# Sketched attention and a multiplicative FFN: the steps behind the sixtieth in another order, with other engines and buffers for some

## The chip, the cores and the metric

One core of a Trainium2 chip runs the whole program. Its engines take instructions in order, each from its own stream: TensorE (PE, and PEld for its weight loads), VectorE (DVE), ScalarE (ACT), GpSimd (POOL) and SyncE (SP), which here issues DMAs. The metric is the device time of one execution in microseconds (us), as the median of the runs shown.

## The reference

```
# attention: q, k, v (4, 4, 1088, 32); S1, S2 (8, 32)
def phi(x):
    a = einsum('rd,bhsd->bhsr', S1, x)
    b = einsum('rd,bhsd->bhsr', S2, x)
    return einsum('bhsi,bhsj->bhsij', a, b).reshape(*x.shape[:-1], 64)
q_p, k_p = phi(q), phi(k)
kv  = einsum('bhsf,bhsd->bhfd', k_p, v)
z   = sum(k_p, axis=2)
num = einsum('bhsf,bhfd->bhsd', q_p, kv)
den = einsum('bhsf,bhf->bhs', q_p, z)[..., None] + 1e-06
x   = (num / den), heads side by side: (4352, 128)
# FFN: w1, w2 (128, 1024), w3 (1024, 1024), w_out (1024, 128)
out = ((x @ w1) * (x @ w2)) @ w3 @ w_out
```

S1, S2 and the weights come as float64 and are read as integer words, from which the program makes float32.

## The kernel before, in words

The work is cut into named steps. A step is a function that issues a few instructions on one engine, and one long string, ORDER, lists all their names. The program calls the steps in that order and then ties each instruction to the one before it on its engine, so that ORDER sets the order on all five engines; an engine waits at an instruction until its data and its buffer are there, and what is behind it waits too. The large loads from SP are tied as well: the fifth is not issued before the first has landed, and so on (UNDER_WAY = 4). A dozen steps named warm are idle matmuls on zeros at the start.

Three more tables go with ORDER. POOL is the set of step names whose elementwise work goes to GpSimd. CPV is the set of copies out of the matmul results that go to VectorE and not to ScalarE. SLOTS says, for each kind of tile, which of its buffers every new tile takes, in the order of the steps; for "x", the three large buffers into which keys (k), values (v) and queries (qh) are loaded, it is one digit for each of these loads.

The names:

- k0 to k3 are the keys of batch 0 to 3. `zero` clears a strip of the key buffer on GpSimd, `load` and `loadr` bring the keys in (lines 560 and 572), `max` is the largest size on ScalarE, `lead` and `rest` (lines 214 and 651) split the keys into two parts, `gram0` to `gram4` are the k Gram products on TensorE (tile ps_g, line 659), followed by small steps on their result (G, T, N, RC), `kp` is the 64-feature product of the keys (line 677), `kv` the product with the values.
- q0 to q3 are 512 queries each, two of them to a batch, q4 and q6 are the 1024 queries of batches 2 and 3, qr the queries left over. `tr` transposes the loaded queries (lines 1000 and 1333), `restT` the left-over ones; then come products (ps_ay, ps_c, ps_cy, ps_a), a split of their results into parts (`sm`, `st`, `sh`, `sl`; s_g, s_t, s_hl), features (ph), and x: ps_xt and ps_xs, copied (`xc`, line 1274) and multiplied into xT (line 1291).
- g0 to g3 are the FFN on 512 tokens of batch 0 and 1 each: `a` is x @ w1 (line 1799), `c` its copy out (line 1804), `b` is x @ w2 (line 1809), `m` the product of both (line 1815), `o` the product with w3o = w3 @ w_out (line 1835; w3o itself is made by f0 to f7, line 534).
- h4 and h6 are the FFN on batches 2 and 3 in a form with seven products for each eight, on 64 x 128 pieces: X, Y, Z (line 1673), elementwise sums (T, m, s, v), P products (128 x 64 pieces, line 1759), and sums of these (k1 to k9, lines 1776 to 1785) with a factor spread by 16 small copies on GpSimd (`ns`, line 1497). gr is the FFN of the tokens left over, 256 columns wide, with its output products at line 1824.
- w1 to w10 are pieces of the weights and of S, loaded (lines 430 to 440) and made float32 in three or four steps each (`c`, `m`, `j`, `a`).

In TensorE's rows a full matmul step is two instructions of 512 columns on the whole 128 x 128 array; X, Y, Z use 64 of its rows, P 64 of its columns, and the k Gram and the query products 32 or 64 rows.

Of the kernel before, what the change touches and what calls it, by code (L numbers as in the profile page):

```python
# [37 lines left out]
        "0123456789aejo96p3ke3rfjo7p5t8g50lfin6q8o4donmgp19fh2og3hi5601au6v4jm8emhubcusv62jgo6olsjs"
        "aolp8s0h8roj26gk1ivl8hb3mcu0a5pn7tfd9qe0umb4p5j1e2tkmgjeno5rcub7tjkume92fka4ud5tkbigpq10lv"
        "e4idunrdbfoedkio782hvo",  # L40
    "q_m": "0110110",
    "raw": "010212120211221",
    "s": "012345671252360063202461521024214",
# [10 lines left out]
    g4.oS g5.oS g6.oS g7.oS h4.0T1 h4.0T2 h4.0T3 h4.0m12 h4.0m22 h4.1T2 h4.1m11 h4.1m12 h4.2m11  # L54
    h4.2m12 h4.2m22 h4.3m11 h4.s2 h4.s4 h6.0T2 h6.0m11 h6.0m12 h6.0m22 h6.1T2 h6.1T3 h6.1m11 h6.1m12
    h6.1m22 h6.2T1 h6.2T4 h6.2m11 h6.3T3 h6.3m11 h6.s1 h6.s2 h6.s4 k0.Nf k0.Nh k0.Nr k0.kp1 k1.Nr
    k1.kp1 k2.kp0 k2.kp1 k2.rest0 k3.kp0 k3.kp1 q0.al q0.p01 q0.phi1 q0.sca q1.al q1.bs q1.p12
    q1.phi q1.sca q2.bs q2.p2 q2.phi0 q2.sc q2.sl q3.al q3.bs q3.p01 q3.p12 q3.p2 q3.phi0 q3.sc
    q4.al q4.bs q4.nn q4.p01 q4.p2 q4.phi0 q4.sl q6.al q6.nn q6.p01 q6.phi1 q6.sc q6.sl qr.al qr.bs
    qr.p12 qr.p2 s.KS s.Pp s.blk s.blkh s.low s.rest  # L60
# [22 lines left out]
q0.al k0.Nf q0.phi0 q0.phi1 q0.A1 q0.smy w1.m1 k1.max q0.sty q0.shy k0.kv3 k0.kv1 k0.kv2 q0.sly s.KS k0.kvr kr1.tr
k0.kvm w1.m0 kr1.kT q0.p01 q1.C0 q1.C1 q0.C1 k0.kzt k2.loadr q0.pt0 q0.C1t q0.scy q0.p2 k0.kz q0.pt1 k0.kvc kr1.ab
k0.kqt q0.p12 q0.dn q0.de q0.rc w1.j0 q0.pc0 q0.pc1 q0.x0 k1.kT0 q0.x1 q0.xs0 q0.xs1 q0.xt0 w1.a0 q1.A0 k2.load
w0.load k1.lead0 q0.xc0 q0.xc1 k0.kq w1.a1 k2.max q0.xt1 k1.ab q0.xT0 q0.xT1 g0.4a q1.load g0.5a q1.sm w0.m1 q1.st
q1.Ct g0.4c g0.4b q1.sh q1.sl k1.rest0 g0.7b w0.c1 g0.7a k1.abt w0.j1 k1.gram0 w0.c0 s.RC q1.scy k1.gram1 kh2.load
q1.sca q2.tr g0.5c q1.al q1.p01 q1.p2 k1.gram2 k1.gram3 kr1.abc k1.gram4 w6.load w0.m0 g0.6b w0.j0 g0.7c g0.7m k1.Gm
q1.p12 k1.Gc g0.0a w2.load w0.a1 q1.dn q1.de q1.rc q1.bs k1.Gt g0.3a k1.Ga k1.T0 k2.kT1 k1.Gb g0.3c q1.restT g0.2a
q1.phi k1.T1 q1.pt0 g0.4m w0.a0 q2.max q2.l2 g0.6a k1.Ta k2.lead0 k2.rest0 g0.1a g0.2c k1.Tc g0.5b q3.tr g0.5m k1.Tb  # L90
q1.pc0 q1.pt1 g0.1b w9.load k1.N0 s.AR q2.l1 q2.rm v3.zero q1.pc1 k1.N1 q1.x g0.6c g0.1c k1.Na k1.Nr k3.zero k2.gram0
g0.1m k2.gram1 k2.gram2 q3.max k2.gram3 g0.0c k2.kT0 k1.Nb q1.xT k2.gram4 q3.l2 k2.ab q2.A0 q2.C0 q2.C1 q3.l1 k1.kp0
v1.zero w9.c k2.abt g1.5a g1.5c g1.1a q2.Ct g1.7a q2.At q3.rm q3.A0 k0.Nr q2.sm q3.C0 q3.C1 k2.Gm v1.loadr q2.st w2.m
q2.sh g1.1c g1.2a k1.kp1 g0.6m q3.Ct g1.0a g1.7b k3.load v1.load g1.5b q3.At k2.Gt k3.loadr w2.c k2.Ga g0.0b w9.j
q2.sl g1.7c w6.c g1.6a k1.kv0 q3.sm k2.Gb w5.load q2.sc q2.al g1.0c k2.Gc g1.7m q2.p01 q3.st k1.kv2 k1.kv3 q3.sh w9.m
k1.kv1 k2.T0 k1.kvr q3.sl q2.p2 k2.T1 q2.p12 q2.dn q2.de g1.4a q2.rc k3.max g0.3b g0.0m g1.1b kh3.load g1.4c k2.Ta
g1.2b q3.sc g1.2c w5.c k2.Tc k1.kvc k1.kqt k1.kq g0.3m q3.p01 g1.6c g1.3a g1.5m g1.3b q2.bs q2.phi0 q2.pT0 g1.2m g1.3c
q2.x q2.load k2.N0 k2.Tb k3.lead0 w9.a1 k2.N1 g1.4b q3.al q3.p2 q3.p12 q2.xT0 g2.5a k3.kT1 g2.5c g2.6a q3.dn q3.de
k2.Na g1.3m g2.4a g2.3a w5.m g2.4b g2.6c k3.rest0 g1.0b k2.Nr q3.rc g1.1m g1.4m g1.6b k2.Nb g0.2b kr1.kp w6.j q4.tr
g2.4c g1.6m w7.load w7.c q3.bs q4.max q2.restT w6.m w5.j w2.j q4.l2 w3.load w9.a0 k3.gram0 k3.gram1 k3.gram2 q3.load  # L100
w7.j q3.phi0 k3.gram3 k3.gram4 g2.2a k3.Gc g2.1a g1.0m w2.a0 g2.6b g2.0a g2.4m g2.1c f6.t w6.a0 w4.load g2.3b w2.a1
g2.2b g2.2c g2.0c w6.a1 g2.1b q3.pT0 k3.Gm g0.2m k3.Gt k3.kT0 v3.load w7.m f6.m w5.a1 w5.a0 g2.3c k3.Ga k3.Gb g2.3m
w7.a0 g2.1m w3.m g2.6m q3.x k3.T0 k3.T1 f2.t w3.c w3.j w8.load g2.0b q3.xT0 g3.1a f6.o k3.Ta g3.0a g3.0b g2.7a g2.7b
q4.l1 w7.a1 q4.rm g3.0c g3.0m g2.5b v3.loadr g3.3a w4.c g2.0m g2.2m g3.1c g2.5m g2.7c g2.7m v2.zero g3.6a k3.Tb
v2.loadr k3.ab f4.t k3.Tc k3.abt w4.j g3.3c w3.a1 q4.A0 q4.C0 q4.C1 q4.At k3.N0 k3.N1 v2.load w3.a0 f0.t k2.kp1 f4.m
w4.m g3.6c q3.restT q6.tr g3.6b g3.6m q4.Ct q4.sm w10.load f0.m k2.kp0 f4.o g3.1b f0.o g3.1m qr.max q6.max k3.kp1
q4.st k2.kv0 w4.a1 k3.kp0 k2.kv3 k2.kv1 k2.kv2 k2.kvr q4.sh qr.l2 k3.kv0 k3.kv1 f3.t k2.kvc k3.kv3 k3.kv2 k3.Na w4.a0
qr.l1 qr.rm q4.sl q4.sc q4.al k3.kvr k3.kvc g3.4a q6.l2 g3.4c g3.4b q4.p01 k3.Nr g3.3b q6.l1 w8.c g3.5a k3.Nb g2.4o
g3.4m f1.t f3.m w10.c k3.kqt g3.5c w8.m g3.3m q4.p2 q6.rm k3.kq f1.m f1.o q6.A0 q6.C0 w10.j q6.C1 g3.1o f3.o w8.j
q4.p12 q6.At g3.2b w10.m q6.Ct q4.dn g3.7a q6.sm q6.st w8.a0 w10.a0 qr.A0 qr.C0 qr.C1 g3.0o g2.1o g3.7c w10.a1 g0.3o  # L110
qr.Ct qr.At q6.sh q4.de g1.4o q4.rc q4.bs g3.5b q4.na w8.a1 f2.m f2.o q6.sl q6.sc g2.3o f7.t qr.sm g3.5m q4.nb q4.nm
g3.2a qr.st g3.2c g1.6o q4.nr q4.ne q4.nn q4.phi0 g0.2o q6.al k2.kqt f5.t g3.2m f5.m f5.o q4.phi1 q4.pT0 g3.7b g3.7m
qr.sh g3.6o f7.m k2.kq g0.4o q4.pT1 f7.o v.s v.t q4.x q4.xT2 q6.p01 g3.4o q6.p2 g2.7o g1.2o q6.p12 qr.sl g0.6o q6.dn
q6.de g1.5o q4.xT0 qr.sc qr.al q6.rc q6.bs q4.xT1 q6.nb q6.na q6.nm q6.nr q6.ne v.1 q6.nn q6.phi0 q4.xT3 q6.phi1 o.S3
q6.pT0 h4.s1 q6.pT1 g0.1o g0.0o g0.5o g0.7o g1.0o h4.s2 g3.5o g0.oT g1.7o q6.x g1.1o g2.5o qr.p01 qr.p2 qr.p12 qr.dn
g3.3o qr.de qr.rc qr.bs qr.phi0 qr.pT0 g3.2o q6.xT0 q6.xT1 q6.xT2 o.S1 g2.2o v.2 g3.7o q6.xT3 qr.x qr.xT0 g1.3o g2.0o
g1.oT g2.6o h4.1a5 g3.oT h4.0b5 h4.0bd h4.0a1 h4.0ac g2.oT h4.s3 h4.0b1 o.S2 h4.0bc h4.1a1 h4.1ac h4.1b1 h4.0b2 h4.0a2
# [1817 lines left out]
```

## Time and profile before

| | us |
|---|---|
| median of 3 runs (lowest, highest) | 245.7 (245.46, 246.02) |
| span of the profiled execution | 244.1 |
| median less that span | 1.6 |
| TensorE busy | 236.2 |
| VectorE busy | 206.7 |
| GpSimd busy | 161.9 |
| ScalarE busy | 123.5 |

The profile is of one execution. It has its span, from the first to the last instruction, and no other time of its own; the times of the runs hold what lies around the span as well. Busy times are sums over the span, so an engine that is busy for 85% can be the one waited for in some stretch. The granted clock was 0.998 of full speed over the span. Rows of the timeline have start, duration, engine, line, operation, output <- input and shapes; in brackets at the end stands the idle time before, and what ended it.

### The profile page before, as it was taken

To read this page: it belongs to the slowest core of one execution; us is meant where nothing else is said; L and a number is where in the kernel's file an instruction comes from. 1 tells how busy PE (TensorE), PEld (TensorE's weight loads), DVE (VectorE), ACT (ScalarE), POOL (GpSimd) and SP (SyncE) were. 2 spreads that over 40 slices of the span, in tenths; PEclk is the share of its full clock that TensorE was granted. 3 is DMA by queue.
4 is the path that set the end of the run, shared out by engine and by line. 5 is a ranking of instruction groups with operands and counts; after the bars stand their busy time and mean duration, and the time that the engine had idled before them with its cause. 6 is when DMAs were issued, how large, how long until landed. Compare 5 with 4: busy or idle time off the path is not lost.

```text
span 244.1 us, 6745 instructions
## 1 busy us (share of the span) xinstructions
PE 236.2 (97%) x2724; PEld 129.8 (53%) x2724; DVE 206.7 (85%) x421; ACT 123.5 (51%) x246; POOL 161.9 (66%) x203
## 2 busy tenths in 40 slices
...
GB/s 201 265 143 325 181 227 190 6 197 224 220 141 251 188 217 190 59 1 3 3 0 0 4 0 3 59 113 3 1 0 0 0 3 0 0 1 3 12 90 93
DMA packets 31935, 22.06 MB, mean 90 GB/s; under 512 B 21280, under 2 KB 26528, under 8 KB 31904
## 3 DMA queue, kind: packets, MB, share of 16 engines
...
q14 instruction: 10, 0.08, 0.1%
...
## 4 chain that ended last, share of the span: by engine, by line
PE 87%; DMA 5%; ACT 2%; POOL 2%; DVE 1%; issue 1%; POOLq 0%; SPq 0%
PE b_ps L1809 12%; PE ps_o L1835 12%; PE ps_X L1673 11%; PE a_ps L1799 11%; PE ps_o L1759 10%; PE ps_w3o L534 6%; PE ps_Y L1673 6%; PE ps_Z L1673 3%; PE ps_g L659 2%; PE ps_x L1527 2%; PE ps_ac L1374 2%; DMA qh<-in_q_dram 2%; DMA k<-in_k_dram 2%; PE ps_or L1824 2%; POOL ph L1208 1%; PE idle_ps L255 1%
## 5 line engine op out<-in xcount | busy, mean ns | idle before, releaser
L1673 PE MATMUL ps_X<-xd,wv 64*128 64x512 f32 x112 | 36.3, 593 | 0.0
L1799 PE MATMUL a_ps<-xT,w 128*128 128x512 f32 (+1 forms) x80 | 36.1, 562 | 0.0
L1809 PE MATMUL b_ps<-xT,w 128*128 128x512 f32 (+1 forms) x80 | 35.6, 555 | 0.0
L1804 ACT COPY ffa<-a_ps 128x512 f32<-128x512 f32 (+1 forms) x38 | 20.1, 540 | 29.2 <-PE a_ps L1799 26.7
L1707 POOL TENSOR_TENSOR hc<-hc 128x512 f32<-128x512 f32 x16 | 20.7, 1304 | 15.7 <-DVE hc L1685 15.5
L1835 PE MATMUL ps_o<-ab,w3o 128*128 128x512 f32 x64 | 29.6, 600 | 0.0
L1680 ACT COPY hc<-ps_X 128x512 f32<-128x512 f32 x38 | 21.3, 590 | 16.1 <-PE ps_X L1673 12.9
L1815 DVE TENSOR_TENSOR ab<-ffa,b_ps 128x512 f32<-128x512 f32 (+1 forms) x40 | 23.9, 623 | 4.9 <-PE b_ps L1809 4.1
L501 POOL TENSOR_TENSOR w3c<-w3c,cv_m 128x512 int32<-128x512 int32 x16 | 21.2, 1344 | 4.2 <-DVE w3c L495 4.1
L1673 PEld LDWEIGHTS ps_X<-xd,wv 64*128 64x128 f32 x112 | 14.9, 186 | 13.1 <-issue 10.9
L1799 PEld LDWEIGHTS a_ps<-xT,w 128*128 128x128 f32 x80 | 14.1, 189 | 13.9 <-issue 8.8
L1809 PEld LDWEIGHTS b_ps<-xT,w 128*128 128x128 f32 x80 | 14.4, 190 | 13.1 <-issue 8.1
L1673 PE MATMUL ps_Y<-xd,wv 64*128 64x512 f32 x48 | 19.7, 594 | 0.0
L1835 PEld LDWEIGHTS ps_o<-ab,w3o 128*128 128x128 f32 x64 | 11.6, 190 | 13.4 <-issue 13.0
L534 PEld LDWEIGHTS ps_w3o<-wo,w3T 128*128 128x128 f32 x128 | 15.3, 192 | 2.4 <-issue 2.4
L534 PE MATMUL ps_w3o<-wo,w3T 128*128 128x128 f32 x128 | 15.7, 276 | 0.0
L1759 PE MATMUL ps_o<-hc,w3o 128*64 128x512 f32 x32 | 15.1, 595 | 0.0
L1759 PE MATMUL ps_o<-tt,ws 128*64 128x512 f32 x32 | 13.7, 594 | 0.0
L1680 ACT COPY hc<-ps_Y 128x512 f32<-128x512 f32 x14 | 8.1, 592 | 9.7 <-PE ps_Y L1673 6.6
L263 ACT ACTIVATE cv_c<-raw 128x1024 f32<-128x1024 f32 (+1 forms) x13 | 13.0, 1014 | 0.0
L1540 ACT COPY xd<-ps_x 64x256 f32<-64x256 f32 x24 | 8.8, 367 | 7.2 <-PE ps_o L1835 6.8
L1497 POOL COPY nz<-nz 32x8 f32<-32x8 f32 x32 | 11.1, 347 | 1.4
...
## 6 DMA issues: line engine op xcount, KB each, us to landing
...
```

Source lines behind the costliest of these rows:

```text
L263: act.activation(dst, hi.bitcast(F32), ACT.Prelu, scale=2.0 ** -112, alpha=-2.0 ** 32)
L501: pool.tensor_tensor(d, d, x["m"][:, i * 512:(i + 1) * 512], ALU.add)
L534: pe.matmul(t["o"], w3T[ko][:, c], wo[:, c], start=c == 0, stop=c == NC - 1)
L1673: pe.matmul(x[bank], stat(j, u)[:, i * 128:(i + 1) * 128], rows(j, u), start=new, stop=True, tile_position=(u * 64, 0), skip_group_check=True)
L1680: cp(n(y))(x[k], x[bank])
L1707: on(f"h{g}.{i}m{k}").tensor_mul(both[0][k], both[0][k], both[1][k])
L1759: pe.matmul(acc_o[bank][half[0]:half[1]], w(i), x(i), start=n == 1, stop=n == (2 if j == 3 else 4), tile_position=(0, half[0]), skip_group ...
L1799: pe.matmul(x["a"][:, :w], w_of(0, c), xT[g][:, c0:c0 + w], start=True, stop=True)
L1804: cp(f"g{g}.{c}{su}c")(x["s"][:, :w], x["a"][:, :w])
L1809: pe.matmul(x["b"][:, :w], w_of(1, c), xT[g][:, c0:c0 + w], start=True, stop=True)
L1815: dve.tensor_mul(ab_sb[g, c][:, c0:c0 + w], x["s"][:, :w], x["b"][:, :w])
L1835: pe.matmul(o_ps[g], w3o[:, c], ab_sb[g, c], start=n == 1, stop=n == NC)
```

## The change

The four tables get new values; no step's code changes, and with one line more in ORDER all line numbers are one higher. The first sixty or so steps stay where they are. Behind them the order is new, made by a search that started from the old order. POOL has 89 names in place of 90: 26 names in, 27 out. CPV has 23 in place of 17. In the diff a row of SLOTS stands for the tables:

```
-    "x": "012012201110",
+    "x": "012012101102",
```

From the fifth tile of this kind on, other loads come to other buffers: the keys of batch 2 took the buffer of the keys of batch 0, and take now the one of the queries of batch 1.

On SP, the first loads behind the keys of batch 1; the rows are loads in the order of issue, k being keys (a whole batch, 128x4x256, and its left-over part, 64x4x32), kh keys with another layout, v values, qh queries, raw weights. Before:

```order
L560 DMA k<-in_k_dram 128x4x256
L572 DMA k<-in_k_dram 64x4x32
L609 DMA kr_436<-in_k_dram 64x4x32 x2
L572 DMA k<-in_k_dram 64x4x32
L560 DMA k<-in_k_dram 128x4x256
L430 DMA raw<-in_moe_w_dram 128x512 x2
L975 DMA qh<-in_q_dram 128x1088
```

And now:

```order
L561 DMA k<-in_k_dram 128x4x256
L573 DMA k<-in_k_dram 64x4x32
L431 DMA raw<-in_moe_w_dram 128x512 x2
L594 DMA v<-in_v_dram 64x4x32
L976 DMA qh<-in_q_dram 128x1088
L602 DMA kh<-in_k_dram 32x1024 x4
L441 DMA raw<-in_moe_w_dram 32x4x256 x4
L573 DMA k<-in_k_dram 64x4x32
L561 DMA k<-in_k_dram 128x4x256
```

The two loads of batch 2's keys stood right behind those of batch 1 and ahead of the queries of batch 1; they stand now behind these queries and two more loads.

On DVE, the rows that end with the first x (xT); ay_C, s_loy, s_pr, s_d, s_rc belong to the first queries, s_g, s_t, s_hl and a second ay_C to the next ones, qT to batch 1's. Before:

```order
L1068 STREAM_TRANSPOSE ay_C_601<-ps_cy 128x128
L1101 TENSOR_TENSOR s_loy<-s_loy,ay_C_601 128x128
L1180 TENSOR_TENSOR s_pr<-s_al,s_loy 128x128
L1184 TENSOR_TENSOR s_pr<-s_pr 128x128
L1189 TENSOR_REDUCE s_d<-s_pr 128x2x16
L1194 SCALAR_TENSOR_TENSOR s_rc<-s_d 128x16
L1198 RECIPROCAL s_rc<-s_rc 128x16
L466 TENSOR_SCALAR w_81<-cv_c 128x2x256
L1274 COPY xc<-ps_xt 128x256 x2
L1291 TENSOR_TENSOR xT<-xc,ps_xs 128x256 x2
```

And now, from the same product on:

```order
L1181 TENSOR_TENSOR s_pr<-s_al,s_loy 128x128
L467 TENSOR_SCALAR w_81<-cv_c 128x2x256
L1185 TENSOR_TENSOR s_pr<-s_pr 128x128
L1334 STREAM_TRANSPOSE qT<-qh 128x512
L1190 TENSOR_REDUCE s_d<-s_pr 128x2x16
L1195 SCALAR_TENSOR_TENSOR s_rc<-s_d 128x16
L467 TENSOR_SCALAR w_81<-cv_c 128x2x256
L1199 RECIPROCAL s_rc<-s_rc 128x16
L980 STREAM_TRANSPOSE qT_rest<-qh 128x64
L1131 STREAM_TRANSPOSE ay_C<-ps_c 128x384
L1158 TENSOR_TENSOR s_hl<-ps_a,s_hl 128x2x128
L1275 COPY xc<-ps_xt 128x256
```

The steps of the next queries (L1131, L1158) and two transposes of batch 1's queries (L1334, L980) have come in ahead of xT; one of the two copies xc has gone to ScalarE. Further up, not shown, the first reductions of the next queries and the second kp of batch 0, from GpSimd, have come in as well.

On PE, the end of the program, where the P products of the last batch (64x512) and the FFN of the tokens left over (128x256 and 128x128) stand. Before:

```order
L1824 MATMUL ps_or<-w3o,ab 128x128 x3
L1759 MATMUL ps_o<-hc,ws 64x512 x2
L1824 MATMUL ps_or<-w3o,ab 128x128
L1799 MATMUL a_ps<-xT,w_81 128x256
L1809 MATMUL b_ps<-xT,w_81 128x256
L1759 MATMUL ps_o<-hc,ws 64x512 x2
L1799 MATMUL a_ps<-xT,w_81 128x256
```

And now:

```order
L1760 MATMUL ps_o<-hc,ws 64x512 x2
L1760 MATMUL ps_o<-tt,w3o 64x512
L1800 MATMUL a_ps<-xT,w_81 128x256
L1825 MATMUL ps_or<-w3o,ab 128x128
L1800 MATMUL a_ps<-xT,w_81 128x256
```

Before, the last P products alternated with work on the whole array; now they stand in one piece, and all of the left-over tokens' work here comes behind them.

More of the change, by code (lines that the diff above doesn't have):

```diff
@@ L29 @@
     "b":
-        "012345670214657210671306537457462512346127340273014526045721472352140327540542370673245716"
-        "210605643174306437107523543106572361507514502371054643535436051532410354273245554744570504"
-        "7734023146507073701426351241254057163771361764573436046273673572571236574127105",
+        "012345670214567201573102637514031624504625406712061547021734756027416053274164053261405360"
+        "512640357104257610727325031425670312567312574160352604127641324763512476324763132713421213"
+        "6472310547236435654263107637360473521232513142172503460504361746713526074153762",
     "k_g": "0101",
     "l":
-        "0123456789a7486797c0864b7705995a34210b38c73b92bc0b4879c146a281ba56271a564b60303643a19ca32c"
-        "c2076b",
-    "m":
[L38 to L43, printed above, removed]
-    "x": "012012201110",
+        "0123456789abc12057483a6c0b9528617a0b417c638c0156b0785c9243864b137894b2630ac78a241965c7a308"
+        "2967ac",
+    "m":
+        "0123456789abcdefghijklmnopqrstuv24013567ca8jblptqio9efgh5cp16s3bua84dmol73sb458a1uf1ns0a1i"
+        "s52ue7bnh4t2p3170vi9eajc5n8sh6gkqlufmordc1hvuk5lmpr3h075tjr2uhvf6pcqd87k03ljmgovfkdhlim51s"
+        "qepu9kdear63tgfmqivj2o",
+    "q_m": "0101010",
+    "raw": "012012021021201",
+    "s": "012345672540137620541730625147637",
+    "x": "012012101102",
 }
@@ L53 @@
 POOL = set("""
[L54 to L60, printed above, removed]
+    g4.oS g5.oS g6.oS g7.oS h4.0T1 h4.0T2 h4.0m11 h4.0m12 h4.0m22 h4.1T2 h4.1T4 h4.1m11 h4.1m12
+    h4.1m22 h4.2T3 h4.2m12 h4.2m22 h4.3T2 h4.3m11 h4.s1 h4.s3 h4.s4 h6.0T1 h6.0T2 h6.0m11 h6.0m12
+    h6.0m22 h6.1T1 h6.1T3 h6.1m11 h6.1m12 h6.1m22 h6.2m11 h6.2m22 h6.3T1 h6.3T4 h6.s1 h6.s2 h6.s3
+    h6.s4 k0.Nf k0.Nh k1.Nr k1.kp0 k2.kp1 k3.kp0 k3.kp1 q0.al q0.p01 q0.phi1 q0.sca q1.al q1.bs
+    q1.p01 q1.phi q1.sca q1.scy q2.al q2.p01 q2.p2 q2.phi0 q2.sc q3.p01 q3.p12 q3.phi0 q4.al q4.nn
+    q4.p01 q4.p12 q4.p2 q4.phi1 q4.sc q6.al q6.nn q6.p12 q6.phi0 q6.sc qr.al qr.bs qr.p01 qr.p12
+    qr.phi0 s.AR s.KS s.Pp s.blk s.blkh s.low s.rest
 """.split())
@@ L83 @@
[L83 to L117, printed above, removed]
@@ new lines @@
+k0.gram1 k0.ab0 k1.load q1.max q0.C0t k1.loadr k0.gram2 k0.gram3 k0.gram4 s.Pp k0.abc1 q0.sha w1.c0 kr0.abc k0.kp1
+q0.sla kr1.tr warm8 kr1.kT k1.tr1 k0.Gm k0.Gt w1.c1 q1.l2 q1.l1 kr0.kp w0.load k0.Gc k0.abc0 k0.Ga k0.T0 q1.rm k1.tr0
+k0.Ta k0.N0 k0.Gb k1.kT1 k0.T1 q0.sca k1.max v0.loadr k0.Tb k0.Tc q1.C0 q1.load q0.al k0.N1 w1.m0 s.KS warm9 warm10
+warm7 k1.kT0 kr1.ab k0.kp0 k0.Na k0.Nh q1.A0 k1.lead0 k0.Nb q0.phi0 k0.Nf q0.A1 w1.m1 k0.kv0 q0.smy kh2.load k0.kv3
+q0.sty q0.C1 k0.kv1 q1.sm k0.kv2 k0.kvr q0.shy q0.phi1 q0.C1t q0.pt0 q1.st k0.kvc q0.p01 q0.sly q0.pt1 s.AR k0.kvm
@@ new lines @@
+k0.kzt q0.pc0 q1.sh q0.scy q0.p2 q1.C1 w1.j1 q0.p12 q2.tr k0.kz q0.dn q0.de q0.pc1 w1.j0 q0.x0 w0.m1 w1.a1 q0.x1 k1.ab
+q0.rc w1.a0 q1.restT q0.xc0 q1.Ct q1.sl q1.sca q0.xs0 q0.xt0 q0.xc1 q0.xs1 q0.xT0 q0.xt1 k0.kqt warm11 q0.xT1 k3.zero
+q2.max q3.tr g0.5b q3.max q1.scy w9.load q1.p01 k1.abt k1.rest0 g0.5a k2.zero g0.7b k0.kq w0.c0 g0.6a k1.gram0
+k2.loadr k2.kT1 k2.load g0.5c w0.m0 w0.c1 w0.j1 k1.gram1 q1.al q1.p2 g0.5m k1.gram2 k1.gram3 s.RC q1.p12 w0.a1 w9.m
+k3.loadr w9.c w0.j0 w7.load k1.gram4 g0.6b k1.Gm g0.2a g0.6c g0.4a k0.Nr k2.max q1.dn k3.load k1.Gc g0.0a q1.de g0.3a
```

88 lines of the change are left out of this document (57 added, 31 removed).

## The prediction

> **What bounds the kernel now.** I read the page's first part, then the busy time by stretch, then the chain of work that ended last, then each engine's rows where TensorE stops. The page's line gives TensorE nearly the whole span, and the stretches (start and end, length, then busy time with instruction counts of PE, PEld, DVE, ACT, POOL, granted clock, DMA share, GB/s) say where it isn't busy:
>
> ```profile
> PE 236.2 (97%) x2724; PEld 129.8 (53%) x2724; DVE 206.7 (85%) x421; ACT 123.5 (51%) x246; POOL 161.9 (66%) x203
> ...
> 10.38:27.27 16.89, 15.24 (x412) 12.53 (x409) 12.85 (x41) 13.29 (x30) 11.06 (x18) 1.00 0.73 224
> 27.42:47.90 20.48, 19.08 (x382) 10.20 (x390) 18.21 (x44) 15.05 (x30) 12.40 (x17) 1.00 0.66 160
> 47.91:240.40 192.49, 192.49 (x1844) 100.03 (x1828) 170.22 (x320) 89.25 (x171) 134.27 (x136) 1.00 0.28 65
> ```
>
> From 47.91 to 240.40 TensorE never stops, at a full clock. There only its own work counts. So the time can move in three places: how early the first FFN product starts (27.42), what TensorE waits for between 27.42 and 47.90 (20.48 − 19.08 = 1.40 us), and what its work behind that costs. The profiled execution's span is 244.1; the median of the runs shown is 245.7, 1.6 above it. I sum against the span and add the 1.6.
>
> The chain (start, duration, work) gives the prices of TensorE's steps:
>
> ```profile
> 44.27 1.56 PE ps_g L659 x75
> 45.83 1.16 issue
> 46.98 0.54 PE ps_g L659 x15
> 49.17 2.77 PE a_ps L1799 x6
> 67.78 3.43 PE a_ps L1799 x8
> 76.47 1.91 PE a_ps L1799 x4
> 159.41 1.72 PE ps_X L1673 x8
> ```
>
> The first three rows are batch 2's k Gram with a stall in it. Of the FFN rows two instructions are one step. A 512-column step on the whole array takes 3.43/4 = 0.86, one on a 64-row half 1.72/4 = 0.43. Where such a row starts behind another tile shape it is longer: 2.77 against 3 × 0.858 = 2.57, and 1.91 against 1.72: 0.2 for leaving and coming back, 0.1 for each switch of shape.
>
> **The change, part by part.** No instruction is added or taken away; 1 step fewer lies on GpSimd and copies change engine. The counts of matmuls of each shape stay, so TensorE's work without switches stays.
>
> *The first FFN product.* It needs the first x, which DVE makes. DVE's rows on the way (idle time before a row, and who ended it, in brackets):
>
> ```profile
> 14.91 0.19 DVE L217 TENSOR_REDUCE G_g<-ps_g 128x1 f32<-128x32 f32 x1 [1.35 <-PE ps_g L659]
> 16.63 1.21 DVE L677 TENSOR_TENSOR kp<-kab 128x1024 f32<-128x1024 f32 x1
> 18.96 0.16 DVE L937 TENSOR_TENSOR RC<-RC,ps_Nr 128x8 f32<-128x8 f32 x1 [0.41 <-PE ps_Nr L912]
> 23.20 0.32 DVE L1068 STREAM_TRANSPOSE ay_C<-ps_cy 128x128 f32<-128x128 f32 x1 [1.38 <-PE ps_cy L1030]
> 25.71 0.74 DVE L1274 COPY xc<-ps_xt 128x256 f32<-128x256 f32 x2
> 26.48 0.79 DVE L1291 TENSOR_TENSOR xT<-xc,ps_xs 128x256 f32<-128x256 f32 x2
> 27.19 0.42 DVE L1137 TENSOR_REDUCE s_g<-ps_a 128x32 f32<-128x256 f32 x1
> 27.64 0.42 DVE L201 SCALAR_TENSOR_TENSOR s_t<-s_g,ps_a 128x256 f32<-128x256 f32 x1
> 27.98 0.57 DVE L1130 STREAM_TRANSPOSE ay_C<-ps_c 128x384 f32<-128x384 f32 x1
> 28.48 0.41 DVE L204 SCALAR_TENSOR_TENSOR s_hl<-s_g,s_t 128x256 f32<-128x256 f32 x1
> 28.92 0.42 DVE L1157 TENSOR_TENSOR s_hl<-ps_a,s_hl 128x256 f32<-128x256 f32 x1
> 32.32 0.70 DVE L1333 STREAM_TRANSPOSE qT<-qh 128x512 f32<-128x512 f32 x1
> 37.03 0.22 DVE L979 STREAM_TRANSPOSE qT_rest<-qh 128x64 f32<-128x64 f32 x1
> ```
>
> From 10.38 to the end of xT at 27.27, DVE works 12.85 and idles 4.04. The change puts ahead of xT what stood behind it or elsewhere: the second kp (1.21 on DVE), the five rows of the next queries (0.42 + 0.42 + 0.57 + 0.41 + 0.42 = 2.24), the transposes of 0.70 and 0.22, and one small copy, taken as the 0.16 of RC's row. One of two xc copies leaves, 0.37. That is 1.21 + 2.24 + 0.92 + 0.16 − 0.37 = 4.16 more. If none of it falls into idle time x is 4.16 later; if all 4.04 are filled, 0.1. I go through the order: kp and the copy now stand ahead of the reduction that waited 1.35, and fill that; rows of the next queries stand ahead of the transpose that waited 1.38, and fill about 1.1; the 0.41 is behind the second kp and goes. So 2.86 are filled, and the first FFN product comes at 27.42 + 1.3 = 28.7: **+1.3**. The kp that DVE takes was 1.94 on GpSimd:
>
> ```profile
> L677 POOL TENSOR_TENSOR kp<-kab 128x1024 f32<-128x1024 f32 x1 | 1.9, 1943 | 0.0
> ```
>
> GpSimd isn't late for xT in either order, so its relief earns nothing there.
>
> *TensorE's own stall.* The 1.16 in the chain is idle time in which TensorE waited for nothing the profile shows, in the middle of batch 2's k Gram. Its like stands at 14.27 (0.41) and 20.35 (0.91). Between the first two lie 124 + 125 instructions, between the second and this one 505 + 505, some records being lost. I take it for a refill of TensorE's instructions every 256:
>
> ```profile
> 14.26:20.34 6.08, 5.17 (x124) 4.26 (x125) 4.78 (x17) 4.49 (x11) 4.12 (x8) 1.00 0.58 186
> 20.35:46.97 26.62, 24.90 (x505) 14.51 (x505) 22.57 (x61) 19.86 (x41) 15.59 (x19) 1.00 0.70 183
> 43.08:46.97 3.89, 2.75 (x149) 1.80 (x139) 3.79 (x12) 3.31 (x7) 0.49 (x3) 1.00 0.02 4
> ```
>
> The last of these stretches is my count of 256 back from the stall (it also counts those still running at its start). A refill thus took 3.9 us with idle DMA (0.02) and 6.1 with busy DMA (0.58), and TensorE stalls where it runs through 256 short instructions in less. The Trainium skill, "Runtime: NRT & Kernel Launch", section Instruction fetch mechanics, says that instructions come in blocks of 256 and that crossing into the next is mostly hidden; the spacing in the trace agrees, the three stalls do not, and by its second half this term of the sum would be 0. The changed order puts long FFN products among that block's short ones: by the rows' durations it lasts some 4.9 us, not 2.75. By the quiet refill nothing of the stall is left (−1.16), by the busy one all of it (6.1 − 4.9 = 1.2, so 0). I take **−0.8**, nearer the quiet end, since few loads are under way then.
>
> *The other wait.* The rest of the 1.40 is one row:
>
> ```profile
> 38.37 0.66 PE L1246 MATMUL ps_ph<-ident,ph 128*128 128x128 f32 x4 [0.24 <-POOL ph L1208]
> ```
>
> This transpose now comes behind batch 2's Gram, long after ph: **−0.25**.
>
> *Switches of shape.* Counted in the two orders from the first FFN product on, 54 become 47: 11 to 7 before the second queries' products, and the rest at the end, where the last batch's P products are no longer cut up. 7 × 0.1 = **−0.7**, between 0 and −1.0 by the longest such rows.
>
> *Batch 2's keys.* Their buffer was batch 0's keys'; now it is the one from which batch 1's queries are transposed. The clearing on GpSimd, and behind it two loads on SP, now wait for the last transpose, which DVE does right behind xT, at about 29.3. Before, SP issued them at 14.95:
>
> ```profile
> 14.95 0.59 SPq L572 DMA_DIRECT2D k<-in_k_dram  x1
> 15.59 0.60 SPq L560 DMA_DIRECT2D k<-in_k_dram  x1
> ...
> DMA to landing us min/median/max: 4.3/4.7/5.5
> ...
> 56.97 1.17 ACT L207 ACTIVATE k_abs<-k 128x1152 bf16<-128x1152 f32 x1
> ...
> 39.51 0.86 DVE L214 TENSOR_SCALAR kk<-k,k_g 128x1152 f32<-128x1152 f32 x1
> ...
> 29.26 1.35 DVE L651 TENSOR_TENSOR kk<-k,kk 128x1152 f32<-128x1152 f32 x1
> ```
>
> Now: clear by 30, issue to 31, landing (4.3 to 5.5) at 35.5 to 36.5, maximum 1.17, a small row of 0.2 as at 14.91, split 0.86 + 1.35: ready at 39.1 to 40.1. TensorE reaches the Gram, which the order has moved ahead of the second x, at 28.7 + 10 FFN steps of 0.86 + 2.1 (1.56 + 0.54) for batch 1's Gram: 39.4. The bounds are 0 and 0.7 at the landing's ends; DVE, waiting in order, holds what stands behind it, so I take **+0.6**. SP issues in order too: w7, k3 and v1 stand behind these loads. By my walk of the order v1 lands at 56 to 57 and is needed near 58.
>
> *The tail.* Before, DVE's last rows are short of work:
>
> ```profile
> 240.60 0.29 DVE L1858 COPY oT<-ps_or 128x128 f32<-128x128 f32 x1 [1.41 <-PE ps_or L1824]
> ```
>
> In the new order the last sums (0.69 each) and the product for the rest tokens stand in one queue, and the rest's output products come about 0.25 late by my walk: **+0.2** (0 to 0.7, one such sum).
>
> Sum: 1.3 − 0.8 − 0.25 − 0.7 + 0.6 + 0.2 = +0.35; 244.1 + 0.35 + 1.6 = 246.05, I say 246.0.
>
> **The rivals.**
>
> *Faster: the cover is complete.* DVE's idle time is filled wholly, x comes 0.1 and not 1.3 later, and the keys land at the early end: 246.05 − 1.2 − 0.6 = 244.25. For it: 4.04 us of idle, nearly all waits for TensorE, whose steps ahead of x are the same set. Against: 4.16 us of work leaves nothing over, and the five rows stand in two groups.
>
> *Slower: batch 2's keys are late.* One of the v loads took 7.2:
>
> ```profile
> DMA to landing us min/median/max: 2.3/3.4/7.2
> ```
>
> With that, the landing is at 38.2, the split is ready at 41.8, TensorE stands 2.3 and not 0.6 at the Gram, and SP hands on the delay: 246.05 + 1.7 = 247.75. It decides from a landing behind 37. For it: w9's four pieces are issued just ahead; against: with the later start fewer loads compete.
>
> *Slower: GpSimd's fan-out at the end.* The 16 small copies took 8.77 once and 3.56 the second time:
>
> ```profile
> 181.62 8.77 POOL L1497 COPY nz<-nz 32x8 f32<-32x8 f32 x16
> ...
> 231.65 3.56 POOL L1497 COPY nz<-nz 32x8 f32<-32x8 f32 x16
> ```
>
> With 8.77 at the end, 5.2 more, some 3 of it before the last outputs need it, the last store is 2.2 late: 248.2.
>
> *The halves.* In the new order 31 of 109 neighbouring X steps are on the same half (26 before), and 19 of 54 P steps (14 before). If such a neighbour had to wait a whole half step, ten more would cost 10 × 0.43 = 4.3: 250.3. The row at 159.41 holds two steps on one half between two on the other and still takes 0.43 each, which speaks against it. The Trainium skill, "TensorEngine Tiling (Array Packing)", Key Properties, says tiles of the array operate independently, from which this would follow; the trace disagrees.
>
> **How the numbers follow.** Forecast 0.38, with its own range 245.4 to 246.6; complete cover 0.31; late keys 0.19; fan-out 0.09; halves 0.03. A change under 0.2% (0.49 us) can't be told from none. Of the forecast 0.25 are the same, 0.10 slower, 0.03 faster; complete cover is faster but for 0.01; the other three are slower. So faster 0.33, same 0.26, slower 0.41. The range: cut at 243.8, below the complete cover with a quarter of it left out (0.08), and at 248.3, which leaves out the halves and a third of the fan-out and of the late keys' tail (0.10).
>
> **What would show it.** The first FFN product at 28.7 (below 27.9: complete cover; above 29.5: I sized DVE's gaps wrongly). No idle "issue" over 0.4 in batch 2's Gram. That Gram's wait for DVE's split 0 to 0.7. TensorE unbroken from there to the end, its rows from the second queries to the end 0.7 shorter. The last copies on GpSimd under 4. Wrong it would be if a wait that shows nowhere in the old trace opens between 50 and 230, above all where SP's loads are handed on late.

## The result and the profile after

The changed kernel takes 247.41 us in the median of 5 runs (246.6 to 248.03), the old one 245.47 beside it (245.22 to 246.02): a ratio of 1.0083, 95% interval 1.0056 to 1.011. It is slower by about 1.9 us. Measured once more later it took 246.9 against 245.35 (1.0074, 1.0041 to 1.0107). The profiled execution has a span of 244.8, 0.7 over that of the old one; it is the fastest of the five, 246.6.

Busy times and the stretches of the changed kernel, to be held against those of the prediction; then the second and third stretch of another execution in the old order (taken from the experiment with the doubled copies below, which differs from the old kernel only at 180 us, in a place where nothing waits):

```profile
PE 237.8 (97%) x2724; PEld 136.2 (56%) x2724; DVE 213.7 (87%) x434; ACT 116.9 (48%) x234; POOL 151.8 (62%) x202
...
10.38:27.27 16.89, 15.38 (x412) 12.46 (x410) 15.20 (x48) 15.69 (x34) 10.35 (x18) 1.00 0.86 249
27.77:46.26 18.49, 18.39 (x382) 10.16 (x390) 17.38 (x44) 16.06 (x30) 9.54 (x14) 1.00 0.91 207
46.27:240.78 194.51, 194.16 (x1843) 106.20 (x1827) 175.24 (x325) 79.19 (x154) 127.36 (x136) 1.00 0.25 58
```

```profile
26.37:46.58 20.21, 19.08 (x382) 10.19 (x390) 17.92 (x44) 15.09 (x30) 12.40 (x17) 1.00 0.73 166
46.59:238.85 192.26, 192.26 (x1842) 99.78 (x1827) 170.38 (x320) 89.03 (x171) 137.10 (x152) 1.00 0.27 64
```

The second stretch runs in both from the first FFN product to the second queries' first product (382 instructions of TensorE), the third from there to the last product. Against this execution of the old order (span 242.8) the first FFN product comes 27.77 − 26.37 = 1.40 later, the second stretch is 1.72 shorter, and the third 2.25 longer: 1.40 − 1.72 + 2.25 = 1.93, the whole difference of the two last products (240.78 and 238.85). So the change gained where the prediction looked for the gain, lost most of that again ahead of it, and lost 2 us where I had said that TensorE's own work alone counts. Two executions are compared here, each the fastest of its runs. Against the old profile that the prediction was summed from, the three are +0.35, −1.99 and +2.02, in sum +0.38: the two old executions differ mainly in the head, by a stall of 0.91 that only one of them has. The 2 us in the third stretch stand in both comparisons.

The chain of waits says where in the long stretch:

```profile
187.25 1.78 POOL tt L1733
189.25 0.55 POOL nz L1498
189.84 0.56 POOL nz L1498
...
194.27 0.20 POOL nz L1498
194.54 1.28 POOL xd L1655
195.86 0.69 PE ps_X L1674
```

Before, TensorE stood in the chain there with nothing but its own products. Now the chain leaves it at 181 and runs over DVE and GpSimd: a sum (h4.3T2), the 16 small copies of `q4.ns`, and one of the sums that batch 3's products need (`h6.s3`). TensorE's row shows the wait as a stretched first product and a small gap (modelled ends hide most of it):

```profile
194.55 1.12 PE L1674 MATMUL ps_X<-xd,wv 64*128 64x512 f32 x2
195.86 0.69 PE L1674 MATMUL ps_X<-xd,wv 64*128 64x512 f32 x1 [0.19 <-POOL xd L1655]
```

The next step starts 1.31 and not 0.43 behind: 0.88 lost. The second profile of this kernel has the same place, 1.34 behind. Taking each step's time to the next one's start, less what such a step takes undisturbed, 176 to 206 holds 2.31 us too much (0.57 before), 50 to 94 2.77 (2.16 before), and all else from 50 on 0.2 less than before. (These are sums over TensorE's rows.)

### The profile page after: what moved, and what is told of

The parts are those of the page before. It is cut to its first block, busy times and chain, and to the rows that moved or that the text cites. A ratio compares the mean times of both kernels' runs of the same rounds, so it can differ in the third digit from the quotient of the medians.

```text
span 244.8 us, 6753 instructions
## 1 busy us (share of the span) xinstructions
PE 237.8 (97%) x2724; PEld 136.2 (56%) x2724; DVE 213.7 (87%) x434; ACT 116.9 (48%) x234; POOL 151.8 (62%) x202
## 4 chain that ended last, share of the span: by engine, by line
PE 86%; DVE 7%; POOL 3%; issue 1%; ACT 0%; DVEq 0%
PE b_ps L1810 13%; PE a_ps L1800 12%; PE ps_X L1674 11%; PE ps_o L1836 11%; PE ps_w3o L535 6%; PE ps_Y L1674 6%; PE ps_o L1760 5%; PE idle_ps L256 3%; PE ps_g L660 3%; PE ps_Z L1674 3%; PE ps_ac L1375 2%; PE ps_x L1528 2%; POOL nz L1498 2%; PE ps_or L1825 2%; PE ps_kv L770 1%
## 5 line engine op out<-in xcount | busy, mean ns | idle before, releaser
L1674 PE MATMUL ps_X<-xd,wv 64*128 64x512 f32 x112 | 40.0, 598 | 0.2 <-POOL xd L1655 0.2
L1805 ACT COPY ffa<-a_ps 128x512 f32<-128x512 f32 (+1 forms) x31 | 16.0, 536 | 40.2 <-PE a_ps L1800 37.5
L1681 ACT COPY hc<-ps_X 128x512 f32<-128x512 f32 x34 | 19.1, 589 | 18.5 <-PE ps_X L1674 16.7
L1708 POOL TENSOR_TENSOR hc<-hc 128x512 f32<-128x512 f32 x17 | 22.3, 1324 | 5.7 <-DVE hc L1686 4.9
L1674 PEld LDWEIGHTS ps_X<-xd,wv 64*128 64x128 f32 x112 | 16.7, 186 | 11.3 <-issue 7.0
L1674 PE MATMUL ps_Y<-xd,wv 64*128 64x512 f32 x48 | 22.3, 593 | 0.0
L1760 PE MATMUL ps_o<-hc,ws 128*64 128x512 f32 x32 | 15.0, 594 | 0.0
L1686 DVE TENSOR_TENSOR hc<-hc,ps_Z 128x512 f32<-128x512 f32 x16 | 10.8, 684 | 1.9 <-PE ps_Z L1674 1.0
L1510 POOL TENSOR_TENSOR ph<-s_al,s_bs 128x1024 f32<-128x1024 f32 (+1 forms) x5 | 8.9, 1779 | 5.4 <-DVE s_bs L1460 5.1
L1422 POOL TENSOR_TENSOR s_hl<-s_hl,ay_C 128x512 f32<-128x512 f32 (+1 forms) x3 | 3.4, 1132 | 13.9 <-DVE AR L955 9.3
```

The lines of the kernel that those rows point to most:

```text
L1674: pe.matmul(x[bank], stat(j, u)[:, i * 128:(i + 1) * 128], rows(j, u), start=new, stop=True, tile_position=(u * 64, 0), skip_group_check=True)
L1681: cp(n(y))(x[k], x[bank])
L1708: on(f"h{g}.{i}m{k}").tensor_mul(both[0][k], both[0][k], both[1][k])
L1760: pe.matmul(acc_o[bank][half[0]:half[1]], w(i), x(i), start=n == 1, stop=n == (2 if j == 3 else 4), tile_position=(0, half[0]), skip_group ...
L1805: cp(f"g{g}.{c}{su}c")(x["s"][:, :w], x["a"][:, :w])
```

## The experiments

**The copies behind the sums.** The 16 copies delay h6.s3; so I moved them behind it and h6.s4.

```
- ... h6.0bc q4.ns h4.3P2 ...  h6.s3 ... h6.s4 gr.1c ...
+ ... h6.0bc h4.3P2 ...  h6.s3 ... h6.s4 q4.ns gr.1c ...
```

> The changed order, with the 16 small copies of the first wide pair (q4.ns, 5.20 us on GpSimd at 189.25) moved behind the two sums h6.s3 and h6.s4 that the last batch's products need. Theory A, the fan-out delays these sums and TensorE with them: the idle 0.19 and the stretched steps at 194.6 (0.89 too long) and 203.9 (0.33) go, the span falls by about 1.3 from 244.8 to 243.5, the median from 247.4 to about 245.5, since the copies' own varying length (8.77, 5.20, 3.56 in the traces so far) no longer counts, and the lowest and highest run come within 0.9 of each other (1.4 now). The copies themselves take near 3.6, since DVE then adds from the matmul results and not within SBUF. Theory B, neighbours on one half of the array cost: nothing changes, 247.4. Theory C, the loss lies in the head or in the loads: nothing changes.

Measured: 247.54 (246.6 to 250.79), ratio 1.0088 (1.0061 to 1.0115). No gain: Theory A in this form fell. h6.s3 is ready in time and that wait is gone, but another one has come. The rows of DVE, GpSimd and TensorE:

```profile
188.70 1.74 DVE L1743 TENSOR_TENSOR tt<-tt,hc 128x512 f32<-128x512 f32 x1 [0.57 <-POOL tt L1733]
190.36 1.75 DVE L1733 TENSOR_TENSOR tt<-hc,tt 128x512 f32<-128x512 f32 x1
...
188.62 1.27 POOL L1655 TENSOR_TENSOR xd<-xd 128x512 f32<-128x512 f32 x1
189.85 1.71 POOL L1660 TENSOR_TENSOR xd<-xd 128x512 f32<-128x512 f32 x1
...
192.16 1.08 PE L1760 MATMUL ps_o<-tt,ws 128*64 128x512 f32 x4 [1.13 <-DVE tt L1733]
```

DVE's sums, 0.68 alone, take 1.74 and 1.75, and each ends 0.55 behind one of GpSimd's (190.44 behind 189.89, 192.11 behind 191.56); GpSimd's second sum takes 1.71 and not 1.27. A P product waits 1.13 for the second of DVE's. The two engines' sums do not run beside each other: this became Theory D. The copies took 4.48, not the 3.6 that I expected. The Trainium skill, "SBUF — State Buffer", section SBUF: two separate sides, says that a port pair is shared by DVE and GpSimd and locked for a whole instruction when DVE's has two operands in SBUF and GpSimd's reads SBUF, the later one standing still. These rows agree. The changed kernel's own rows show both sides: a DVE sum within SBUF takes 1.48 beside GpSimd's, and sums with an operand from the matmul results (ps_o) keep their 0.69:

```profile
185.70 1.48 DVE L1728 TENSOR_TENSOR tt<-hc 128x512 f32<-128x512 f32 x1
...
195.17 0.69 DVE L1785 TENSOR_TENSOR oc<-oc,ps_o 64x512 f32<-64x512 f32 x1
...
185.35 1.27 POOL L1738 TENSOR_TENSOR hc<-hc 128x512 f32<-128x512 f32 x1 [3.60 <-DVE tt L1728]
...
194.54 1.27 POOL L1655 TENSOR_TENSOR xd<-xd 128x512 f32<-128x512 f32 x1
```

**One sum ahead.** Only h6.s3 is moved, into GpSimd's idle time ahead of h4.2T3.

```
- ... h4.2m12 h4.2T3 ...  h4.k2 h6.s3 h4.2P6 ...
+ ... h4.2m12 h6.s3 h4.2T3 ...  h4.k2 h4.2P6 ...
```

> The changed order, with only h6.s3 moved, into the 3.6 us in which GpSimd idles ahead of h4.2T3; the 16 copies and h6.s4 behind them stay. Theory A: h6.s3 is ready at 183 and not at 195.8, the step at 194.6 is no longer stretched; h6.s4 comes 1.27 earlier, at 195.8, and is needed at 198.6, so it waits only if the copies take over 8 us. Span about 243.6, median 245.5 to 246.0. Theory B or C: no change, 247.4.

Measured: 246.75 (245.31 to 248.4), ratio 1.0069 (1.0035 to 1.0103), not clearly below the changed kernel's 1.0083. The stretch at 194.6 is gone, as said; but a DVE sum beside the moved one takes 1.45, and the P product behind the one at 184.18 starts at 185.08, 0.47 late:

```profile
182.00 1.27 POOL L1655 TENSOR_TENSOR xd<-xd 128x512 f32<-128x512 f32 x1
...
182.37 1.45 DVE L1738 TENSOR_TENSOR hc<-hc 128x512 f32<-128x512 f32 x1
```

GpSimd's idle time was not free: DVE pays for what is put there.

**The copies twice, in the old order.**

```
- for t in range(4):
+ for t in [*range(4)] * (2 if key == 4 else 1):
```

> The order before, with the 16 copies of the first wide pair done twice (the second time with the same values). Theory A, what counts is the place and not the length: GpSimd idles for 7.8 us behind h6.s4 there, h6.s4 would come at about 196 where it is needed at 198.9; the time stays within 0.3 of 245.5. Rival, GpSimd's work counts as such: 3.6 to 8.8 us more copies show as 1 us or more.

Measured: 245.36 (244.57 to 247.35), ratio 1.0012 (0.999 to 1.0034). The 32 copies took 13 us and cost nothing, since h6.s4 behind them still ended 4 us before GpSimd had anything else to do. In the old order that place has slack; its length doesn't matter.

```profile
180.29 12.98 POOL L1497 COPY nz<-nz 32x8 f32<-32x8 f32 x32
193.35 1.27 POOL L1659 TENSOR_TENSOR xd<-xd 128x512 f32<-128x512 f32 x1
198.58 2.65 POOL L1707 TENSOR_TENSOR hc<-hc 128x512 f32<-128x512 f32 x2 [3.96 <-DVE hc L1685]
```

**Part of the change alone, and that part undone.** Three steps that the change put on GpSimd, h4.2T3, h4.3T2 and h6.s3: taken back to DVE in the changed kernel, put on GpSimd in the old one. Orders stay.

```
  POOL (changed kernel)
- h4.2T3 h4.3T2 h6.s3
  POOL (old kernel)
+ h4.2T3 h4.3T2 h6.s3
```

> The changed order, with three elementwise steps off GpSimd and on DVE, where the old tables had them: h4.2T3, h4.3T2 and h6.s3 (order untouched). Theory D, from the two moved fan-outs: DVE's sums and GpSimd's sums that both read two operands from SBUF do not run beside each other (DVE rows of 0.68 took 1.74 beside GpSimd's 1.27), so at 182 to 196 a sum on GpSimd costs DVE 0.8 to 1.1 where it costs 0.60 on DVE itself. Then DVE's rows there are all 0.68 to 0.69, h6.s3 is ready by 192, the stretched step at 194.6 (0.89) goes, no P product waits over 0.3, the 16 copies run from 181.8 on, and the median falls by 0.8 to 1.5 from 247.5 to 246.0 to 246.7. Rival, GpSimd is the relief it was meant to be: DVE gets 1.8 more in its queue, the sums h4.k2 to k9 come later, and the time stays or rises.

> The order before, with the same three steps put on GpSimd: one part of the change alone. Theory D: DVE rows beside them stretch to over 1.2, the copies of q4.ns start at about 188 and not at 181, the last batch's product that needs h6.s3 waits 0.5 to 1.5, the median rises by 0.7 to 1.5 over the time before. Rival: DVE is relieved of 1.8, no change or a gain of up to 0.5.

Measured: in the old kernel 245.98 (245.26 to 247.44) against 245.04, ratio 1.0038 (1.0015 to 1.0061): this one part of the change costs 0.9 us by itself (0.4 to 1.5), inside the 0.7 to 1.5 of Theory D. In the changed kernel 246.73 (245.57 to 248.44), 1.0068 (1.0038 to 1.0098): the gain of 0.7 at best is within the noise of the two ratios, so the median doesn't show it. The rows do. The old kernel's DVE and GpSimd with the three steps moved:

```profile
182.45 1.76 DVE L1732 TENSOR_TENSOR tt<-hc,tt 128x512 f32<-128x512 f32 x1
187.99 1.76 DVE L1707 TENSOR_TENSOR hc<-hc 128x512 f32<-128x512 f32 x1
...
182.07 1.59 POOL L1737 TENSOR_TENSOR hc<-hc 128x512 f32<-128x512 f32 x1 [1.15 <-DVE tt L1727]
187.42 1.78 POOL L1732 TENSOR_TENSOR tt<-hc,tt 128x512 f32<-128x512 f32 x1 [3.76 <-DVE tt L1727]
```

And DVE in the changed kernel with the three taken back, where no sum takes over 0.71 between 182 and 191:

```profile
187.60 0.69 DVE L1733 TENSOR_TENSOR tt<-hc,tt 128x512 f32<-128x512 f32 x1
188.21 0.68 DVE L1738 TENSOR_TENSOR hc<-hc 128x512 f32<-128x512 f32 x1
```

There the stretch at 194.6 is gone, a P product waits 0.61 in its place, and the time from the first FFN product to the last is 240.44 − 28.52 = 211.92, against 240.78 − 27.77 = 213.01 in the changed kernel: 1.1 less in one execution each. That execution had started its first FFN product 0.75 later.

Not all came as Theory D had it. In the old kernel no product waited for h6.s3, where 0.5 to 1.5 was expected; the one wait of TensorE there is 0.4, for a DVE sum (h4's T4, line 1742). In the changed kernel 0.61 and not at most 0.3 is left at a P product. Counted as above, 176 to 206 holds 1.1 us too much in the old kernel with the three steps on GpSimd (0.57 without), and 1.5 in the changed one with them on DVE (2.31 without): they are 0.5 to 0.8 of the 1.74 that the change loses there. The rest I did not take apart.

**The second kp back on GpSimd.**

```
  POOL
+ k0.kp1
```

> The changed order, with the second product of batch 0's key features (k0.kp1) back on GpSimd, 1.20 us less on DVE ahead of the first x. By the prediction's step, x is bound by DVE's work and comes 1.2 us earlier: first FFN product at 26.6 and not 27.8, time 0.5 to 1.2 less. Rival, DVE's idle time takes up the work: TensorE waited 0.50 for ScalarE's xs and only 0.34 for xT; the first FFN product moves by less than 0.4, and the time by less than 0.4 either way.

Measured: 247.68 (246.51 to 248.5), ratio 1.01 (1.0072 to 1.0128): no gain. The first FFN product stands 18.33 behind the first k Gram product, as with the kp on DVE (18.23). DVE waits instead, for TensorE; it idled 0.81 there in the changed kernel:

```profile
15.93 0.29 DVE L825 COPY krT<-ps_krt 128x128 f32<-128x128 f32 x1 [1.82 <-PE ps_krt L820]
```

So this 1.21 of the 4.16 that I had counted fell into idle time, as the prediction had it.

**Thinning DVE ahead of x, three tries.** First four rows moved behind x:

```
- w1.j1 q0.p12 q2.tr ...  w1.a0 q1.restT q0.xc0 q1.Ct q1.sl q1.sca ...  q0.xT1 k3.zero
+ w1.j1 q0.p12 ...  w1.a0 q0.xc0 ...  q0.xT1 q2.tr q1.restT q1.Ct q1.sl q1.sca k3.zero
```

> The changed order, with four DVE rows and their follower (q2.tr 0.70, q1.restT 0.18, q1.Ct 0.53, q1.sl 0.39, and q1.sca on GpSimd) moved from ahead of the first x to behind it. By the prediction's first term, x comes earlier by what TensorE's transposes allow: first FFN product at 27.0 to 27.3 and not 27.8 (18.2 behind the first k Gram product; 16.8 to 17.9 in the old order), and 0.4 to 0.8 of the time. Rival: x is bound by ScalarE's and TensorE's chain, not by DVE's rows, the product moves by less than 0.2; or batch 1's keys and queries come later by as much as x comes earlier, and the time stays.

Measured: 250.56 (248.93 to 252.31), 1.0211 (1.0167 to 1.0255), clearly slower. I had moved a row that TensorE waits for: q1.Ct reads the result buffer that the kq transposes (of batch 0's kv result) take next. Nor did x come earlier: it ends 18.04 behind the first k Gram product, 18.09 in the changed kernel. The reciprocal that x needs is no earlier there (a small row ahead of it, s_rc, took 0.77 and not 0.29 beside a GpSimd sum), and behind it DVE waits 0.76 for TensorE's ps_xs, which waits for ScalarE's xs: for x the first rival held.

```profile
29.00 0.69 PE L806 MATMUL ps_kq<-ident,kvc 128*128 128x128 f32 x2 [1.82 <-DVE ay_C L1131]
```

The second try left q1.Ct, moved kr1.kT to ScalarE and the weight rows w1.j1 and w1.j0 behind the reciprocal and behind x; alone, and with the three steps on DVE:

```
- q1.restT q0.xc0 q1.Ct q1.sl q1.sca ...  q0.xT1
+ w1.j1 w1.a1 q0.xc0 q1.Ct ...  q0.xT1 w1.j0 w1.a0 q1.restT q1.sl q1.sca q2.tr
```

> The changed order, with DVE's rows ahead of the first x thinned again: the copy kr1.kT on ScalarE, one weight row (w1.j1 with w1.a1 on GpSimd) behind the reciprocal that x needs and the other (w1.j0, w1.a0), q1.restT, q1.sl, q2.tr behind x; q1.Ct, whose result buffer TensorE needs, stays ahead. The prediction's first term, x waits for DVE: the reciprocal ends at 14.9 behind the first k Gram product (16.2 in the changed order), the first FFN product comes at 17.0 to 17.4 behind it (18.2), and the median falls by 0.6 to 1.1 from 247.4. Rival, the loss of the head comes from elsewhere (TensorE's own order, ScalarE): 18.0 or later, no change. Second rival: x is earlier, but the weight rows moved behind it are late for the second product, a wait of 0.5 to 1 takes the gain.

> Both repairs at once: the thinned head, and h4.2T3, h4.3T2, h6.s3 on DVE. If the two are what the change lost, and independent, the median is 247.4 less 0.7 (measured for the three steps) less 0.6 to 1.1: 245.6 to 246.1, within 0.9 of the time before. If something else of the size of 1 us is lost, it stays at 246.7.

> The changed kernel once more, beside its repairs on one chip: 247.0 to 247.6, first FFN product 18.2 to 18.3 behind the first k Gram product, the step at 194.6 stretched by 0.9.

Measured: 249.07 (248.84 to 251.42) alone, 248.2 (246.76 to 251.48) with the three steps, 246.9 (246.3 to 250.7) for the changed kernel beside them. The first is slower again (1.0159, 1.0114 to 1.0205); the second, 1.0093 (1.0058 to 1.0128), is no gain and can't be told from the changed kernel's 1.0074. In the second x does end earlier, 17.27 behind the first k Gram product and not 18.09, but the first FFN product stands at 19.0. The second rival had it right: the products wait for a weight row, and the last idle matmul for the result buffer that q1.sl frees. The waits of TensorE in the first of the two, where a load of keys (kh) came late besides, so that x isn't earlier in that execution:

```profile
PE ps_kv L770 <- DMA kh<-in_k_dram: 1.5, 1, 1.5
PE idle_ps L256 <- DVE s_hl L1158: 1.3, 1, 1.3
...
PE b_ps L1810 <- POOL w L471: 0.5, 1, 0.5
```

The third try moved less (q1.restT and q2.tr behind x, kr1.kT to ScalarE, both weight rows just behind the reciprocal), with the three steps on DVE:

```
- w1.j1 q0.p12 q2.tr ...  q0.rc w1.a0 q1.restT q0.xc0 q1.Ct q1.sl q1.sca ...  q0.xT1
+ q0.p12 ...  q0.rc w1.j1 w1.a1 q0.xc0 q1.Ct q1.sl w1.j0 w1.a0 q1.sca ...  q0.xT1 q1.restT q2.tr
```

> As the two repairs at once, but with a smaller one at the head, which leaves ahead of x what TensorE waits for on the way: q1.Ct and q1.sl (their result buffers go to kq and to the last idle matmul) and both weight rows, now behind the reciprocal; only kr1.kT (to ScalarE), q1.restT and q2.tr leave. If x waits for DVE, the first FFN product comes at 17.5 to 17.8 behind the first k Gram product (18.25 in the changed order, 19.0 in the first try), TensorE waits for no weight row, and the median is 246.0 to 246.4, that is 0.3 to 0.7 under the three steps alone (246.7). If x doesn't, it stays at 18.2 and 246.7.

Measured: 247.41 (246.17 to 249.42), 1.0103 (1.0066 to 1.014), no gain. The reciprocal ends 1.25 earlier, at 24.51, but x at 27.50 and not at 27.63, and 18.06 against 18.09 behind the first k Gram product: the rows that now stand between fill the difference. The first FFN product waits 1.44 for a weight row of GpSimd and stands 18.48 behind:

```profile
27.91 0.70 PE L1810 MATMUL b_ps<-xT,w 128*128 128x512 f32 x1 [1.44 <-POOL w L471]
```

So x came clearly earlier in one of the four runs alone, and there the weight rows of DVE and GpSimd and a result buffer were late in its place. I found no repair for it. That these rows are what costs the head its 1.4 is argued from the waits and not shown by a faster run; which of them do stays open.

**The refill.** 16 of the 27 idle matmuls at the start taken away, so that all that follows stands 32 instructions earlier.

```
- WARM = [27, 2, 3, ...
+ WARM = [11, 2, 3, ...
```

> The order before, with 16 fewer idle matmuls at the very start (11 for 27), 32 instructions fewer ahead of everything. If the idle time called issue is a refill every 256 instructions, it moves 16 matmuls later in the program: in batch 2's k Gram it stood behind the 75th and 15 before the last of that chain piece, and would now come at about the last of the Gram or just behind it; in batch 0's Gram it moves 16 matmuls on as well. Rival, it belongs to the place (data or a result buffer): it stays where it was. The first products may start earlier or later by a few tenths, since TensorE idles less long; the time is not what this tells.

Measured in one execution (253.08; the head alone is 7 us later): the chain cuts batch 2's Gram now 84 : 5 by a stall of 1.30, and not 75 : 15 by one of 1.16.

```profile
14.91 1.17 PE ps_g L659 x58
16.08 0.57 issue
21.87 3.24 issue
51.30 1.73 PE ps_g L659 x84
53.03 1.30 issue
54.33 0.37 PE ps_g L659 x5
```

The chain counts only part of the Gram's 144 instructions. In TensorE's own rows the stall stands behind 122 of them in the three other executions of the old order and behind 138 here: 16 later, as expected, and in batch 0's Gram behind 99 and not 83. In all four, 1701 of the recorded instructions of TensorE stand ahead of the stall in batch 2. So it goes with the count of instructions, as a refill every 256 does, and not with data or a result buffer. The refill ahead of the kv products took 3.24 there. In the other executions of the old order that same refill cost 0.91, 0.63 and nothing. The 7 us in the head, with late loads of the keys and a granted clock of 0.986, are not what this run tells.

## Why the prediction was right, and where it wasn't

The range, 243.8 to 248.3, held the 247.41, and slower was the likeliest sign, with 0.41. The number itself, 246.0, is 1.4 short, and a large part of the reason lies in a place for which the sum had no term. That the range held was luck in good part. Of the 0.41 for slower 0.19 stood on late keys, which were not late. Against the profile that the sum started from, the span grew by 0.7 where +0.35 was forecast, but by errors that cancel: the head and the keys were put 1.55 too high, and the 2 us of the third stretch were missing. And the prediction's own sign of being wrong came true: a wait that shows nowhere in the old trace opened at 194.6, between 50 and 230. Its steps, with what they measured:

- *First FFN product, +1.3.* It came at 27.77 and not at 28.7, +0.35 in the two profiles compared. But the old profile held a refill of 0.91 and DVE's wait of 1.38 behind it that the old order doesn't always have: in three executions its first FFN product stands 17.9, 17.3 and 16.8 behind the first k Gram product, in the changed order 18.2 to 18.3 in six. Against the last of these, which has no refill there, it is +1.4, against the second +0.9. So +1.3 was too big against the profile that I summed from, where 27.77 is by the prediction's own sign (below 27.9) the complete cover, and about right against one of three executions; which of them is usual, three don't show. The work was put too high: up to the end of x, DVE is busy for 15.55 of 17.25 now and was for 12.85 of 16.89, 2.70 more and not 4.16, in part because rows that follow each other without a wait overlap (the one at 25.79 starts 0.07 before the one at 25.68 has ended). Idle time fell from 4.04 to 1.7, so 2.3 were filled and not 2.86: 0.81 is left of the wait of 1.35, none of the 1.38, 0.10 of the 0.41.
- *Refill, −0.8.* All 1.16 went: no profile of the changed order has a stall over 0.2 in batch 2's Gram. *The other wait, −0.25:* gone. Of the 1.72 by which the second stretch is shorter, 1.03 are waits (1.13 to 0.10) and 0.69 is TensorE's busy time (19.08 to 18.39), in which switches of shape are counted too.
- *Switches, −0.7.* Steps with an excess of about 0.1 fell from 50 to 43, 4.96 to 4.25 us in sum: −0.71.
- *Batch 2's keys, +0.6.* Wrong, it cost nothing. SP issued the loads at 28.3 and 28.9, not at 30.5 to 31, since the transpose that frees the buffer (27.56 to 28.25) and the clearing came sooner, and TensorE went from its products into the Gram at 38.54 without a wait. (In the rival of late keys, 41.8 against 39.4 is 2.4 and not 2.3.)

```profile
27.56 0.69 DVE L1334 STREAM_TRANSPOSE qT<-qh 128x512 f32<-128x512 f32 x1
28.92 0.64 SPq L561 DMA_DIRECT2D k<-in_k_dram  x1
38.54 0.34 PE L660 MATMUL ps_g<-kk 128*32 128x64 f32 x8
```

- *Tail, +0.2.* Two waits, 0.28 at the last P product and 0.23 at the rest tokens' first product: +0.5.
- *What was missing.* "There only its own work counts", said of 47.91 to 240.40. That held for the old order and was carried over to the new one without a check of who feeds TensorE at 176 to 206: 1.74 more lost there, and 0.6 at 50 to 94, which I did not take apart further. The fan-out rival had the right part, the 16 copies with sums behind them, but put it at the end (there they took 3.54, beside DVE sums of matmul results) and not at its first place, where the new order starts them at 189.25 and not at 181.62. It also took their length for one that happens to vary; it goes with what DVE does: a copy takes 0.18, and one that meets a DVE sum within SBUF 0.55 to 1.10. Of the 1.74, 0.5 to 0.8 is shown to come from three steps on GpSimd, by moving them in both kernels; the cause of the rest is open.
- *The halves.* No sign: from 156 to 176, all X, Y and Z products, the steps exceed 0.43 by 0.01 in sum, before and after, though by the order about a quarter of the neighbours there share a half. The P products show why:

```profile
188.62 0.59 PE L1760 MATMUL ps_o<-hc,ws 128*64 128x512 f32 x1
188.62 0.64 PE L1760 MATMUL ps_o<-hc,w3o 128*64 128x512 f32 x1
...
189.48 0.59 PE L1760 MATMUL ps_o<-tt,ws 128*64 128x512 f32 x1
```

The order has h4.3P3 and h4.2P5 on the upper half and then h4.2P2 on the lower. By their operands the rows are h4.3P3, h4.2P2 and h4.2P5: the lower half's product starts with the first of the upper half's, ahead of the second that stands before it in the order. Each half works through its own products, so a neighbour on the same half costs nothing as long as the other half has work. The prediction's row at 159.41 thus doesn't disagree with the halves' independence; it only shows that the wait doesn't follow from it.

Not shown: why the changed kernel's runs spread more (246.3 to 250.7 in 12 runs, against 244.4 to 246.9). Refills that differ by up to 3 us in the head would do it, but neither of the kernel's two profiles, both of executions at 246.6 and below, has one.
